# One written schedule for a whole attention and two-expert-layer kernel, counts loaded one expert ahead, and other PSUM banks for the transposes

## Chip, cores and metric

The kernel runs on one core of one Trainium2 chip. The metric is the device time of one execution in microseconds (us), lower is better. The core's engines are named as in the profile: PE (matmuls; PEld is its weight loads), DVE (vector), ACT (scalar), POOL and SP. Each takes its own list of instructions in order, and waits at semaphores that the others raise.

## The reference

```python
# 1. chunked attention (2 batches, 8 heads, 576 rows, head size 64, chunks of 64 rows)
#    softmax(q k^T / 8) v inside each chunk; out as x of 1152 rows of 512
# 2. mixture of 8 experts, one expert for each row
logits = x @ w_gate
expert_idx = np.argmax(logits, axis=1)
...
for i in range(N):
    e = expert_idx[i]
    if counts[e] < capacity:      # capacity = 1152 // 8 * 2 = 288
        disp[e, counts[e]] = x[i]
...
h = np.maximum(np.einsum('ecd,edf->ecf', disp, w1), 0.0)   # 512 -> 1024
y = np.einsum('ecf,efd->ecd', h, w2)                       # 1024 -> 512
out[i] = gate_w[i] * y[expert_idx[i], pos[i]]              # kept rows only, else 0
# 3. four domain experts, every row through each, mixed by domain_probs
for e in range(E):
    h = np.maximum(x @ w1[e], 0.0)
    out += p[:, e:e + 1] * (h @ w2[e])
```

## The kernel before

**Three stages.** The attention stage works through nine tiles of 128 rows and ends with the routing: DVE computes for every expert how many rows it keeps, the lists of row numbers for the gathers (`gidx`), and a row of 17 whole numbers `ovi`: the count of all kept rows, a form for each of eight experts in the order in which they are worked on, and the column at which each expert's rows start. The expert stage (`expert`, `block`) works on one expert after the other. The dense stage (`dense`) sends all rows through the four domain experts.

**Forms and blocks.** How many rows an expert has is known only at run time, so each expert has three blocks of code: block 1 for rows 128 to 255 (form above 2), block 2, called the small block here, for up to 64 rows (form 2 or 3), and block 0 for the first 128 rows, always run. Blocks 1 and 2 stand under `tc.If` (lines 677, 682 and 683), and the next expert under line 728. Every engine takes these branches by itself, from a register loaded from `ovi` by `numbers` (line 549). An engine that skips a block adds to its semaphore what the block would have added, after its own earlier work has ended.

**One block.** All weights and activations are split in a high and a low part (ACT makes the high part, DVE subtracts it from the source to get the low one) and multiplied in three products. On PE a block is: `first(0)`, the 512-wide first layer of one half of the hidden units; half of `first(1)`; `turn(0)`, which transposes the first half by matmuls with the identity; the rest of `first(1)`; `second(0)`, the second layer, which reads `ht`, the turned half after ACT (high, line 596) and DVE (low, line 597); `turn(1)`; the rest of `second`; then the result is turned again (`ty`) and put into `x2`. The turns go through PSUM tiles of the tag `tp`, with two buffers for all blocks; `ys2` are two accumulators, `pg0` one bank for each kind of block, `pg1` one for all: 2 + 2 + 3 + 1 = 8 banks.

**Around the blocks.** `late(k)` ends the splitting of the expert's own second-layer weights: two casts on ACT (line 115) and four subtractions on DVE (`part_lo`, line 119), ahead of the expert's first branch. Between the steps of block 0 the lists in `also` split the next expert's weights, load the one after it, and turn the next expert's gathered rows (`xprep`, lines 538 to 546), through `pg0[1]`, `pg0[2]` and `pg1` (line 701). For the first expert `xprep` runs ahead of its blocks and uses `tp`, `pg0[0]` and `pg1` (line 663).

**What sets the order.** A region under `tc.manual_schedule` is issued as written on the engines it names; outside such a region a scheduler chooses. The attention stage has a region of its own (line 128, all engines), the expert stage one (line 520) and the dense stage one (line 735), the latter two for PE, ACT, DVE and SP.

Of the kernel before, what the change touches and what calls it, by code (L numbers as in the profile page):

```python
# [71 lines left out]
def kernel(ctx: ExitStack, tc: tile.TileContext, kqv_d, wg, w_all, dp, cst, out, cap):  # L72
# [3 lines left out]
    XW = 2 * P + 64  # L76
    assert cap <= XW

    dpool = ctx.enter_context(tc.tile_pool(name="dpool", bufs=1, space=DRAM))
    x_d = dpool.tile([NTOK, DM], F32, name="x_d")  # L80
    meta_d = dpool.tile([NTOK, MC], F32, name="meta_d")
# [43 lines left out]
    with ExitStack() as ast:  # L125
        ap_ = ast.enter_context(tc.tile_pool(name="attn", bufs=2))
        ps = ast.enter_context(tc.tile_pool(name="aps", bufs=1, space=PSUM))
        ast.enter_context(tc.manual_schedule())


        wz = ap_.tile([P, 512], F16, bufs=1, name="wz")
# [385 lines left out]
    def w2(h, part, ff):  # L517
        return hls[2 * h + 1][:, part, ff * DM:(ff + 1) * DM]

    with ExitStack() as est, tc.manual_schedule(engines={ENG.PE, ENG.Activation, ENG.DVE, ENG.SP}):  # L520
        hp_ = est.enter_context(tc.tile_pool(name="mh", bufs=2))
        xtp = est.enter_context(tc.tile_pool(name="mx", bufs=1))
        ps = est.enter_context(tc.tile_pool(name="mps", bufs=1, space=PSUM))

        ys2 = [ps.tile([P, DM], F32, name=f"y{j}") for j in range(2)]


        pg0 = [ps.tile([P, FH], F32, name=f"pg0{j}") for j in range(3)]
        pg1 = ps.tile([P, FH], F32, name="pg1")
        xts = [xt0, xtp.tile([P, 2 * KD * XW], F32R, name="xt1")]  # L530
        xbig = [x[:, 0:4 * KD * P].rearrange("p (a k n) -> p a k n", a=2, k=KD) for x in xts]
        xsmall = [x[:, 4 * KD * P:].rearrange("p (k a n) -> p k a n", a=2, k=KD) for x in xts]
# [5 lines left out]
        def xprep(k, kd, t):  # L538
            for w in range(2):
                nc.tensor.transpose(t[:, w * P:w * P + P], xrs[k % 2][:, w, kd * P:kd * P + P], ident)  # L540
            hi_lo(xbig[k % 2][:, 0, kd], xbig[k % 2][:, 1, kd], t[:, 0:2 * P])
# [6 lines left out]
        def numbers(src, **kw):  # L548
            return nc.values_load_multi_w_load_instructions(src, min_val=0, **kw)[1]

        kept, *form_r = numbers(ovi[0:1, 0:1 + NE], max_val=NTOK)
        o_r = numbers(ovi[0:1, 1 + NE:1 + 2 * NE], engines=(ENG.Activation, ENG.DVE), max_val=NTOK)
        regs = []

        def load(k, j, h):
# [4 lines left out]
        def block(k, w, also=()):  # L560
# [2 lines left out]

            lo, n = wins[w]
            both = n < P
            y = ys2[w % 2]
            hs, ht = {}, {}
            pg = (pg0[w], pg1)

# [19 lines left out]
                nc.scalar.copy(hs[h], pg[h])  # L589

            def turn(h):
                tp = ps.tile([P, NF, n], F32, tag="tp", bufs=2, name="tp")
                for j in range(NF):
                    turned(tp[:, j], hs[h][:, j * P:j * P + P])
                ht[h] = hp_.tile([P, NF, 2, n], F32R, tag="h", name="ht")
                nc.scalar.activation(out=ht[h][:, :, 0], in_=tp, func=ACTF.Relu)  # L596
                nc.vector.scalar_tensor_tensor(out=ht[h][:, :, 1], in0=tp, scalar=0.0, in1=ht[h][:, :, 0].bitcast(F32),  # L597
                                               op0=ALU.max, op1=ALU.subtract)
# [23 lines left out]
            place(4)  # L622
            second(1, range(NF))
            yr = hp_.tile([P, DM], F32, tag="ys", bufs=1, name="yr")
            ty = ps.tile([P, KD, n], F32, tag="tp", bufs=2, name="tp")
            for j in range(2):
                nc.scalar.copy(yr[:, j * 256:j * 256 + 256], y[:, j * 256:j * 256 + 256])
            place(5)
# [22 lines left out]
        def expert(k):  # L651
# [3 lines left out]
            if k == 0:  # L655
                gather(0, (2,))
                gather(1)

                nc.gpsimd.memset(x2[:, :, :, P:NTOK].bitcast(F32), 0.0)
                for h in range(2):  # L660
                    part_lo(0, h)
                for kd in range(KD):
                    xprep(0, kd, ps.tile([P, 512], F32, tag="tp", bufs=2, name="tp") if kd < 2 else (pg0[0], pg1)[kd - 2])
                for h in range(2):
                    part_lo(2, h)
                places()
                regs.extend(numbers(pli[0:1, :], engines=(ENG.SP,), max_val=NE + NDOM - 1))
                chores = list(dense_rows())
                for h in range(2):
                    part_lo(1, h)  # L670
                for j in (0, 2, 1):
                    for h in range(2):
                        load(1, j, h)
            elif k + 2 < NE:
                gather(k + 2)
            late(k)
            with tc.If(form_r[k] > 2):
                block(k, 1)
            if k == 0:
# [18 lines left out]

            def nxt(i, kd):
                if k + 1 < NE:  # L700
                    t = pg1 if len(turns) == KD else pg0[1 + len(turns) % 2]
                    turns.append(t)
                    also[i].append(lambda: xprep(k + 1, kd, t) if kd < KD else xprep_small(k + 1, t))

# [17 lines left out]
            assert len(chores) <= 20  # L722
            block(k, 0, also)
            if k == 0:
                scatter(meta_d, [(posi[:, i:i + 1], meta[:, i]) for i in range(NT)], [])
                nc.gpsimd.dma_start(out=mcol, in_=meta_d.rearrange("(i p) c -> p i c", p=P))
            if k + 1 < NE:
# [4 lines left out]
        late(NE)  # L732


    with ExitStack() as est, tc.manual_schedule(engines={ENG.PE, ENG.Activation, ENG.DVE, ENG.SP}):
        accp = est.enter_context(tc.tile_pool(name="accp", bufs=1))
        hp_ = est.enter_context(tc.tile_pool(name="dh", bufs=2))
        ps = est.enter_context(tc.tile_pool(name="dps", bufs=4, space=PSUM))
# [130 lines left out]
        def pick_last(ws):  # L869
            if len(ws) == 1:  # L870
                return dense(ws[0])
            with tc.If(kept <= LAST + ws[0]) as few:  # L872
                dense(ws[0])
            with few.Else():
                pick_last(ws[1:])
# [46 lines left out]
```

## Time and profile before

| | |
|---|---|
| median of 3 runs | 619.68 us (617.58 to 619.73) |
| the profiled execution | 620.28 us, its span 618.1 us |
| PE busy | 579.5 us, 94% of the span |
| DVE, ACT busy | 296.1 us, 200.9 us |
| mean granted clock of PE | 0.975 of full speed |
| start of the dense stage on PE | 240.21 us |

The profiled execution's time is 2.2 us more than its span, which runs from the first to the last recorded instruction. Routing ends at about 59 us, the expert stage runs to 240 us. With these inputs six experts have rows. In the order worked on their blocks are: 1 and 0; 1, 2 and 0; 0; 2 and 0; 2 and 0; 0. They are called experts 0 to 5 below.

### The profile page before, as it was taken

What the parts mean: (1) busy time and instruction counts of PE and PEld (TensorE: products, weight loads), DVE (VectorE), ACT (ScalarE), POOL (GpSimd) and SP (SyncE); (2) the same over time, 40 slices, a digit from 0 to 9 for tenths busy, and PEclk for the clock granted to TensorE, in tenths of its full rate; (3) what the DMA queues carried; (4) which work ended last, traced back from release to release, by engine and by line L of the source; (5) the groups of instructions that cost most, each with busy time, mean ns of one, the idle gap of its engine ahead of it and who ended that gap; (6) DMA issues with size and microseconds to landing.
All of it is one profiled execution on the core that took longest, in us unless ns stands there. A gap on an engine that the chain in (4) does not pass through costs nothing.

```text
span 618.1 us, 8796 instructions
## 1 busy us (share of the span) xinstructions
PE 579.5 (94%) x3376; PEld 503.6 (81%) x3376; DVE 296.1 (48%) x576; ACT 200.9 (32%) x394; POOL 71.5 (12%) x63
## 2 busy tenths in 40 slices
PE   6998699998797988999999999999999999999995
PEld 3785577776676767989989989989989989989984
DVE  4897828147445376242462452452452452454221
ACT  4785237267454476111211211211211211211110
POOL 3311813202202050000000000000000000000032
PEclk8997799999898999999999999999999999999998
DMA  8782286428727176400120120120220000000022
GB/s 326 258 286 75 60 315 202 114 73 296 262 69 249 46 233 200 186 1 1 68 69 1 68 69 1 69 68 1 69 68 1 2 1 1 1 0 1 1 83 76
DMA packets 17322, 61.36 MB, mean 99 GB/s; under 512 B 2720, under 2 KB 2864, under 8 KB 16624
## 3 DMA queue, kind: packets, MB, share of 16 engines
q1 hardware_dynamic: 14544, 52.95, 25.1%
q0 software_dynamic: 2720, 7.66, 4.1%
q8 instruction: 33, 0.54, 0.4%
q14 instruction: 25, 0.20, 0.1%
HBM read 55.86 MB, written 4.75 MB: 98 GB/s over the span
## 4 chain that ended last, share of the span: by engine, by line
PE 59%; issue 1%; POOL 1%; DVE 0%; POOLq 0%
PE pg L768 30%; PE po L797 20%; PE po L816 8%; POOL out L500 1%; PE po L831 0%; DVE xr L804 0%; POOLq L872 0%; POOLq L500 0%
## 5 line engine op out<-in xcount | busy, mean ns | idle before, releaser
L768 PE MATMUL pg<-x,hl 128*128 128x384 f32 (+1 forms) x1152 | 187.5, 322 | 1.6 <-DVEq L728 1.6
L768 PEld LDWEIGHTS pg<-x,hl 128*128 128x128 f32 x1152 | 184.5, 188 | 3.1 <-issue 1.8
L797 PE MATMUL po<-hl,h 128*128 128x512 f32 (+1 forms) x588 | 137.4, 392 | 0.0
L797 PEld LDWEIGHTS po<-hl,h 128*128 128x128 f32 x588 | 108.6, 188 | 24.6
L119 DVE TENSOR_TENSOR hl<-raw,hl 128x1024 fp32r<-128x1024 f32 x80 | 95.3, 1219 | 24.0 <-ACT hl L115 20.2
L778 ACT ACTIVATE h<-pg 128x384 fp32r<-128x384 f32 x64 | 31.5, 492 | 186.1 <-PE pg L768 185.8
L115 ACT CAST hl<-raw 128x1024 fp32r<-128x1024 f32 x80 | 82.2, 1056 | 0.9 <-DVEq L728 0.9
L779 DVE SCALAR_TENSOR_TENSOR h<-pg,h 128x384 fp32r<-128x384 f32 x64 | 35.6, 557 | 94.2 <-ACT h L778 94.2
L574 PE MATMUL pg<-hl,xt 128*128 128x512 f32 x240 | 65.4, 421 | 3.2 <-PEq L682 1.6
L574 PE MATMUL y<-hl,ht 128*128 128x512 f32 x240 | 65.0, 412 | 1.6 <-DVE ht L597 1.6
L804 DVE SCALAR_TENSOR_TENSOR xr<-po,mcol,xr 128x512 f32<-128x512 f32 (+1 forms) x43 | 31.7, 737 | 59.7 <-PE po L797 59.0
L574 PEld LDWEIGHTS pg<-hl,xt 128*128 128x128 f32 x240 | 45.9, 200 | 14.6 <-issue 5.3
L574 PEld LDWEIGHTS y<-hl,ht 128*128 128x128 f32 x240 | 43.7, 192 | 13.4 <-DVE ht L597 4.4
L816 PE MATMUL po<-h,hl 128*128 128x288 f32 x384 | 51.9, 295 | 0.0
L816 PEld LDWEIGHTS po<-h,hl 128*128 128x128 f32 x384 | 51.3, 189 | 0.0
L775 ACT CAST h<-pg 128x288 fp32r<-128x288 f32 x32 | 12.8, 400 | 97.9 <-DVE pg L773 97.9
L400 POOL DMA_INDIRECT xr<-x_d,gidx x24 | 28.2, 1174 | 127.8 <-PE pg L540 95.4
L825 POOL MEMSET raw<- 128x512 f32 x1 | 0.5, 527 | 268.4 <-DVE hl L119 268.4
L597 DVE SCALAR_TENSOR_TENSOR ht<-tp,ht 128x512 fp32r<-128x512 f32 (+1 forms) x22 | 13.6, 616 | 28.5 <-ACT ht L596 28.4
L822 DVE TENSOR_TENSOR rest<-po,rest 128x288 f32<-128x288 f32 x28 | 12.8, 458 | 26.6 <-PE po L816 26.6
L773 DVE SCALAR_TENSOR_TENSOR pg<-pg,xt 128x288 f32<-128x288 f32 x32 | 22.1, 690 | 1.6 <-PE pg L768 1.6
L776 DVE TENSOR_TENSOR h<-pg,h 128x288 fp32r<-128x288 f32 x32 | 14.7, 459 | 15.4 <-ACT h L775 15.4
(158 smaller groups left out, 393.6 us busy)
## 6 DMA issues: line engine op xcount, KB each, us to landing
raw<-in_w_all SPq DMA_DIRECT2D x72, 512.0 KB, 4.1
kqv<-in_kqv SPq DMA_DIRECT2D x8, 768.0 KB, 8.1
raw<-in_w_all SPq DMA_DIRECT2D x4, 1024.0 KB, 5.7
x_d<-x SPq DMA_DIRECT2D x9, 256.0 KB, 3.1
xt<-meta_d SPq DMA_DIRECT2D x1, 1056.0 KB, 8.5
kqv<-in_kqv SPq DMA_DIRECT2D x3, 256.0 KB
xr<-x_d,gidx POOLq DMA_INDIRECT x24
cc<-in_cst SPq DMA_DIRECT2D x1, 373.5 KB
```

The costliest lines, as they stand in the source:

```text
L115: nc.scalar.copy(hls[j][:, 0, a:b], raws[j][:, a:b])
L119: nc.vector.tensor_tensor(out=hls[j][:, 1, a:b], in0=raws[j][:, a:b], in1=hls[j][:, 0, a:b].bitcast(F32), op=ALU.subtract)
L400: nc.gpsimd.indirect_dma_start(out=xrs[k % 2][0:n, w, :], out_offset=None, in_=x_d[:, :], in_offset=bass.IndirectOffsetOnAxis(ap=ix, axis=0))
L574: nc.tensor.matmul(o, t(a), wt(b), start=start and i == 0, stop=stop and i == len(pairs) - 1)
L768: nc.tensor.matmul(pg[:, 0:n], w1(u % 2, a, kd)[:, ff * P:ff * P + P], x2[:, b, kd, g * GW:g * GW + n], start=c == 0, stop=c == 3 * KD - 1)
L773: nc.vector.scalar_tensor_tensor(out=hs, in0=hs, scalar=0.0, in1=domain(u // NH), op0=ALU.max, op1=ALU.mult)
L776: nc.vector.tensor_tensor(out=h[:, ff, 1, 0:n], in0=hs, in1=h[:, ff, 0, 0:n].bitcast(F32), op=ALU.subtract)
L778: nc.scalar.activation(out=h[:, ff, 0], in_=pg[:, 0:GW], func=ACTF.Relu)
L779: nc.vector.scalar_tensor_tensor(out=h[:, ff, 1], in0=pg[:, 0:GW], scalar=0.0, in1=h[:, ff, 0].bitcast(F32), op0=ALU.max, op1=ALU.subtract)
L797: nc.tensor.matmul(po, h[:, ff, a, tt * P:tt * P + P], w2(u % 2, b, ff)[:, cols], start=c == 0, stop=c == 3 * NF - 1)
L804: nc.vector.scalar_tensor_tensor(out=acc[t][:, cols], in0=po, scalar=pe, in1=acc[t][:, cols], op0=ALU.mult, op1=ALU.add)
L816: nc.tensor.matmul(po[:, 0:W], w2(u % 2, b, ff)[:, d * P:d * P + P], h[:, ff, a, 0:W], start=c == 0, stop=c == 3 * NF - 1)
```

## The change

Four things are changed. One `manual_schedule` for PE, ACT, DVE and SP spans the whole kernel (POOL keeps one in the attention stage). The registers are loaded with the numbers of one expert at a time: the form of expert 0 ahead of the stage, then `count(k + 1)` behind `late(k)` inside expert `k`, one load on every engine and a second one on ACT and DVE; the count of kept rows is loaded behind expert 0's block 0. The PSUM tiles: three `tps`, one for each kind of block, take `turn(0)` and `ty`; `turn(1)` reuses the block's own `pg0`; one accumulator `y` serves all: 3 + 3 + 1 + 1 = 8 banks. `xprep` for the next expert uses `pg0[1]`, `pg0[2]`, `tps[1]`, `tps[2]` and `pg1`, and for expert 0 `tps[0]`, `tps[2]`, `pg0[0]` and `pg1`.

```diff
@@ -76,6 +76,7 @@
     XW = 2 * P + 64
     assert cap <= XW
 
+    ctx.enter_context(tc.manual_schedule(engines={ENG.PE, ENG.Activation, ENG.DVE, ENG.SP}))
     dpool = ctx.enter_context(tc.tile_pool(name="dpool", bufs=1, space=DRAM))
     x_d = dpool.tile([NTOK, DM], F32, name="x_d")
     meta_d = dpool.tile([NTOK, MC], F32, name="meta_d")
@@ -125,7 +126,7 @@
     with ExitStack() as ast:
         ap_ = ast.enter_context(tc.tile_pool(name="attn", bufs=2))
         ps = ast.enter_context(tc.tile_pool(name="aps", bufs=1, space=PSUM))
-        ast.enter_context(tc.manual_schedule())
+        ast.enter_context(tc.manual_schedule(engines={ENG.Pool}))
 
 
         wz = ap_.tile([P, 512], F16, bufs=1, name="wz")
@@ -517,16 +518,17 @@
     def w2(h, part, ff):
         return hls[2 * h + 1][:, part, ff * DM:(ff + 1) * DM]
 
-    with ExitStack() as est, tc.manual_schedule(engines={ENG.PE, ENG.Activation, ENG.DVE, ENG.SP}):
+    with ExitStack() as est:
         hp_ = est.enter_context(tc.tile_pool(name="mh", bufs=2))
         xtp = est.enter_context(tc.tile_pool(name="mx", bufs=1))
         ps = est.enter_context(tc.tile_pool(name="mps", bufs=1, space=PSUM))
 
-        ys2 = [ps.tile([P, DM], F32, name=f"y{j}") for j in range(2)]
 
 
         pg0 = [ps.tile([P, FH], F32, name=f"pg0{j}") for j in range(3)]
+        tps = [ps.tile([P, 512], F32, name=f"tp{j}") for j in range(3)]
         pg1 = ps.tile([P, FH], F32, name="pg1")
+        y = ps.tile([P, DM], F32, name="y")
         xts = [xt0, xtp.tile([P, 2 * KD * XW], F32R, name="xt1")]
         xbig = [x[:, 0:4 * KD * P].rearrange("p (a k n) -> p a k n", a=2, k=KD) for x in xts]
         xsmall = [x[:, 4 * KD * P:].rearrange("p (k a n) -> p k a n", a=2, k=KD) for x in xts]
@@ -548,8 +550,15 @@
         def numbers(src, **kw):
             return nc.values_load_multi_w_load_instructions(src, min_val=0, **kw)[1]
 
-        kept, *form_r = numbers(ovi[0:1, 0:1 + NE], max_val=NTOK)
-        o_r = numbers(ovi[0:1, 1 + NE:1 + 2 * NE], engines=(ENG.Activation, ENG.DVE), max_val=NTOK)
+        kept = []
+        form_r = [*numbers(ovi[0:1, 1:2], max_val=4)]
+        o_r = [0]
+
+        def count(k):
+
+            form_r.extend(numbers(ovi[0:1, 1 + k:2 + k], max_val=4))
+            o_r.extend(numbers(ovi[0:1, 1 + NE + k:2 + NE + k], engines=(ENG.Activation, ENG.DVE), max_val=NTOK))
+
         regs = []
 
         def load(k, j, h):
@@ -563,7 +572,6 @@
 
             lo, n = wins[w]
             both = n < P
-            y = ys2[w % 2]
             hs, ht = {}, {}
             pg = (pg0[w], pg1)
 
@@ -589,7 +597,7 @@
                 nc.scalar.copy(hs[h], pg[h])
 
             def turn(h):
-                tp = ps.tile([P, NF, n], F32, tag="tp", bufs=2, name="tp")
+                tp = (tps, pg0)[h][w][:, 0:NF * n].rearrange("p (f n) -> p f n", f=NF)
                 for j in range(NF):
                     turned(tp[:, j], hs[h][:, j * P:j * P + P])
                 ht[h] = hp_.tile([P, NF, 2, n], F32R, tag="h", name="ht")
@@ -622,7 +630,7 @@
             place(4)
             second(1, range(NF))
             yr = hp_.tile([P, DM], F32, tag="ys", bufs=1, name="yr")
-            ty = ps.tile([P, KD, n], F32, tag="tp", bufs=2, name="tp")
+            ty = tps[w][:, 0:KD * n].rearrange("p (d n) -> p d n", d=KD)
             for j in range(2):
                 nc.scalar.copy(yr[:, j * 256:j * 256 + 256], y[:, j * 256:j * 256 + 256])
             place(5)
@@ -660,7 +668,7 @@
                 for h in range(2):
                     part_lo(0, h)
                 for kd in range(KD):
-                    xprep(0, kd, ps.tile([P, 512], F32, tag="tp", bufs=2, name="tp") if kd < 2 else (pg0[0], pg1)[kd - 2])
+                    xprep(0, kd, (tps[0], tps[2], pg0[0], pg1)[kd])
                 for h in range(2):
                     part_lo(2, h)
                 places()
@@ -674,6 +682,8 @@
             elif k + 2 < NE:
                 gather(k + 2)
             late(k)
+            if k + 1 < NE:
+                count(k + 1)
             with tc.If(form_r[k] > 2):
                 block(k, 1)
             if k == 0:
@@ -698,7 +708,7 @@
 
             def nxt(i, kd):
                 if k + 1 < NE:
-                    t = pg1 if len(turns) == KD else pg0[1 + len(turns) % 2]
+                    t = (pg0[1], pg0[2], tps[1], tps[2], pg1)[len(turns)]
                     turns.append(t)
                     also[i].append(lambda: xprep(k + 1, kd, t) if kd < KD else xprep_small(k + 1, t))
 
@@ -722,6 +732,7 @@
             assert len(chores) <= 20
             block(k, 0, also)
             if k == 0:
+                kept.extend(numbers(ovi[0:1, 0:1], max_val=NTOK))
                 scatter(meta_d, [(posi[:, i:i + 1], meta[:, i]) for i in range(NT)], [])
                 nc.gpsimd.dma_start(out=mcol, in_=meta_d.rearrange("(i p) c -> p i c", p=P))
             if k + 1 < NE:
@@ -732,7 +743,7 @@
         late(NE)
 
 
-    with ExitStack() as est, tc.manual_schedule(engines={ENG.PE, ENG.Activation, ENG.DVE, ENG.SP}):
+    with ExitStack() as est:
         accp = est.enter_context(tc.tile_pool(name="accp", bufs=1))
         hp_ = est.enter_context(tc.tile_pool(name="dh", bufs=2))
         ps = est.enter_context(tc.tile_pool(name="dps", bufs=4, space=PSUM))
@@ -869,7 +880,7 @@
         def pick_last(ws):
             if len(ws) == 1:
                 return dense(ws[0])
-            with tc.If(kept <= LAST + ws[0]) as few:
+            with tc.If(kept[0] <= LAST + ws[0]) as few:
                 dense(ws[0])
             with few.Else():
                 pick_last(ws[1:])
```

DVE, from the end of the routing to expert 0's first rows. `ovi` is the row of 17 numbers, `gp` and `gidx` make the gather lists, `over` is the routing's last PSUM read, `hl` the split weights, `xt` expert 0's turned rows. Before:

```order
L440 TENSOR_TENSOR dt<-tsb 128x8
L549 TENSOR_LOAD ovi
L918 BRANCH_PREFETCH_HINT
L441 TENSOR_TENSOR dt<-dt,thr 128x8
L442 TENSOR_TENSOR tsb<-tsb,dt 128x8
L549 TENSOR_LOAD ovi
L119 TENSOR_TENSOR hl_91<-raw_87,hl_91 128x1024
L443 TENSOR_TENSOR gp<-tsb,sel 128x192
L119 TENSOR_TENSOR hl_91<-raw_87,hl_91 128x1024
L445 TENSOR_REDUCE gidx<-gp 128x24
L447 TENSOR_TENSOR over<-n_ps,st 128x8
L536 TENSOR_TENSOR xt_71<-tp,xt_71 128x256 x2
```

The same place of the change:

```order
L441 TENSOR_TENSOR dt<-tsb 128x8
L442 TENSOR_TENSOR dt<-dt,thr 128x8
L443 TENSOR_TENSOR tsb<-tsb,dt 128x8
L444 TENSOR_TENSOR gp<-tsb,sel 128x192
L446 TENSOR_REDUCE gidx<-gp 128x24
L448 TENSOR_TENSOR over<-n_ps,st 128x8
L551 TENSOR_LOAD ovi
L120 TENSOR_TENSOR hl_93<-raw_89,hl_93 128x1024 x2
L538 TENSOR_TENSOR xt_73<-tp_1010,xt_73 128x256
```

The two loads and the two weight subtractions have moved behind `over`, and of the loads one is left here.

PE, the small block of an expert past the first, with the semaphores waited for; `pg`, `tp` and `y` are the PSUM tiles. Before:

```order
L574 MATMUL pg_1012<-hl_93,xt_71 128x512 x3
L578 MATMUL tp<-cc,hs 128x64 [waits DVE_49,Activation_49]
L578 MATMUL tp<-cc,hs 128x64 x3
L574 MATMUL pg_1012<-hl_93,xt_71 128x512 x4
L574 MATMUL y_1007<-hl_92,ht 128x512 [waits DVE_49]
```

And in the change:

```order
L582 MATMUL pg_1013<-hl_95,xt_73 128x512 x3
L586 MATMUL tp_1012<-cc,hs 128x64 [waits Activation_49]
L586 MATMUL tp_1012<-cc,hs 128x64 x3
L582 MATMUL pg_1013<-hl_95,xt_73 128x512 x4
L582 MATMUL y<-hl_94,ht 128x512 [waits DVE_49]
```

`turn(0)` (lines 578 and 586) no longer waits for DVE; the first product of `second(0)` still does.

DVE in the change, from an expert's `late` to its first branch; line 120 is `part_lo`, line 551 the loads of the next expert's numbers, line 605 the low part of `ht`:

```order
L120 TENSOR_TENSOR hl_94<-raw_90,hl_94 128x1024 x2
L120 TENSOR_TENSOR hl_96<-raw_92,hl_96 128x1024 x2
L551 TENSOR_LOAD ovi
L929 BRANCH_PREFETCH_HINT
L551 TENSOR_LOAD ovi
L687 COMPARE_AND_BRANCH
L605 SCALAR_TENSOR_TENSOR ht<-tp_1011,ht 128x4x128
```

Before, the four subtractions were followed by the branch at once, and the hint stood ahead of them. PE has one such load between line 739 (728 before) and its hint.

## Rows read from the trace of the kernel before

**Rows 1.** The profile's page: engines; the chain that ended last, its first PE step.

```profile
PE 579.5 (94%) x3376; PEld 503.6 (81%) x3376; DVE 296.1 (48%) x576; ACT 200.9 (32%) x394; POOL 71.5 (12%) x63
...
240.21 16.88 PE pg L768 x96
```

**Rows 2.** Waits of PE from 58 to 241 us: us in total, times, longest.

```profile
PE tp L540 <- DVE over L447: 5.0, 1, 5.0
PE tp L578 <- DVEq L677: 4.5, 2, 2.3
...
PE tp L580 <- DVEq L682: 2.7, 2, 1.4
```

**Rows 3.** Stretches with one small block each: experts 1, 3 and 4.

```profile
core 0: us, PE busy (x) PEld busy (x) DVE busy (x) ACT busy (x) POOL busy (x), PEclk, DMA share, GB/s
...
114.70:126.30 11.60, 11.06 (x57) 8.46 (x57) 1.54 (x3) 3.18 (x7) 0.00 (x0) 1.00 0.07 25
...
158.60:174.20 15.60, 12.78 (x57) 9.74 (x57) 6.08 (x7) 4.63 (x9) 2.48 (x2) 0.89 0.59 190
...
189.60:206.70 17.10, 14.31 (x57) 11.14 (x57) 6.08 (x7) 4.57 (x9) 2.41 (x2) 0.80 0.53 176
```

**Rows 4.** Timeline of PE, small blocks: start, us, instruction, idle before and releaser.

```profile
119.66 1.20 PE L574 MATMUL y<-hl,ht 128*128 128x512 f32 x4
...
164.21 1.76 PE L578 MATMUL tp<-cc,hs 128*128 128x64 f32 x8 [2.27 <-DVEq L677]
...
167.58 1.21 PE L574 MATMUL y<-hl,ht 128*128 128x512 f32 x4
...
198.69 1.91 PE L574 MATMUL y<-hl,ht 128*128 128x512 f32 x4
```

**Rows 5.** DVE's branch at line 677 in expert 3 (window 157.5 to 169 us).

```profile
L677 DVEq COMPARE_BRANCH  x1: 56/56/56, 160.7 to 160.7; - x1
L677 DVEq EVENT_SEMAPHORE  x1: 21/21/21, 164.0 to 164.0; - x1
```

**Rows 6.** Expert 2, block 0: DVE's low part and PE's second layer.

```profile
148.89 0.69 DVE L597 SCALAR_TENSOR_TENSOR ht<-tp,ht 128x512 fp32r<-128x512 f32 x1
...
149.74 1.64 PE L574 MATMUL y<-hl,ht 128*128 128x512 f32 x6
```

**Rows 7.** Register loads: ns min/median/max, first and last start in us.

```profile
L549 DVEq TENSOR_LOAD <-ovi x2: 1119/1500/1880, 59.6 to 61.1; - x2
L549 SPq TENSOR_LOAD <-ovi x1: 767/767/767, 59.6 to 59.6; - x1
L549 PEldq TENSOR_LOAD <-ovi x1: 1042/1042/1042, 59.6 to 59.6; - x1
...
L364 SPq TENSOR_LOAD <-e0i x1: 533/533/533, 26.7 to 26.7; - x1
```

**Rows 8.** Timeline of PE, expert 0.

```profile
56.45 4.85 PE L138 MATMUL w_ps<-wz 128*128 128x512 f16 x11
66.31 1.09 PE L540 MATMUL tp<-cc,xr 128*128 128x128 f32 x4 [5.01 <-DVE over L447]
...
77.77 1.43 PE L574 MATMUL y<-hl,ht 128*128 128x512 f32 x5 [1.41 <-DVE ht L597]
```

**Rows 9.** Timeline of DVE, the same stretch.

```profile
63.09 1.22 DVE L119 TENSOR_TENSOR hl<-raw,hl 128x1024 fp32r<-128x1024 f32 x1 [1.82 <-issue]
...
69.03 2.35 DVE L119 TENSOR_TENSOR hl<-raw,hl 128x1024 fp32r<-128x1024 f32 x2
...
77.03 0.68 DVE L597 SCALAR_TENSOR_TENSOR ht<-tp,ht 128x512 fp32r<-128x512 f32 x1
```

**Rows 10.** Busy tenths of the DMA engines, 56 to 76 us in slices of 0.5 us.

```profile
DMA  0000000456872000000000000000230638856052
```

**Rows 11.** Timeline of PE, start of expert 1.

```profile
100.54 4.48 PE L574 MATMUL pg<-hl,xt 128*128 128x512 f32 x18
...
107.26 1.44 PE L574 MATMUL y<-hl,ht 128*128 128x512 f32 x5 [0.17 <-DVE ht L597]
```

## The prediction

> **What bounds the kernel now.** First the page: PE is busy for 94% of the span, and the chain that ended last runs on PE from the first dense matmul at 240.21 us [rows 1]. In the dense stage PE has no gaps that the change could close: its instructions there are the same before and after. So I look only at what lies ahead of 240.21 us, and there at PE's waits, since PE is the engine that the others feed. Three of them count [rows 2]: 5.0 us once, expert 0's first transposes (line 540) waiting for DVE to pass line 447, the routing's last read of PSUM; 4.5 us in two, `turn(0)` of the small blocks (line 578) waiting for DVE's branch at line 677; and 2.7 us in two, `turn(0)` of block 0 in experts 2 and 5 (line 580) waiting for DVE's branch at line 682. The table by stretches shows what the second kind costs in all: the same small block takes 11.60 us in expert 1, where nothing stalls, 15.60 in expert 3 and 17.10 in expert 4 [rows 3]. [...]
>
> **The small blocks, experts 3 and 4.** `tp` was shared with a block that was skipped, so `turn(0)` waited until DVE had skipped it too; with a bank for each kind of block this wait is gone. What is late next is the low part of `ht` on DVE, which `second(0)` needs. DVE's sequencer reaches its branch at 160.7 us, but counts the block as skipped only when the four subtractions of `late` are through, at 164.0 [rows 5]. Then ACT's high part and DVE's low part follow, each on 256 columns and so below the 0.69 us that DVE takes for 512 [rows 6]; with the hand-overs I take 1.1 us for both. So `second(0)` can start at 165.1, 6.5 us after the block's start. PE itself is there earlier: its start, plus one register load, plus the 4.96 us of expert 1 (114.70 to 119.66) [rows 3, 4], makes 164.3. Against 167.58 that is 2.5 us in expert 3, and, with the same 6.5 us from 189.60, 196.1 against 198.69, so 2.6 us in expert 4. The rest of the block takes 6.6 us in experts 1 and 3 and 8.0 in expert 4 (198.69 to 206.70) [rows 3, 4]; with no stall long enough to lower the clock expert 4 gets 1.4 of this back. Sum 6.5 us; bounds 3 (the clock falls all the same) and 7.2 (PE's path alone decides).
>
> **Block 0 of experts 2 and 5.** The same wait goes, 2.7 us in sum, but I cost it at nothing. In expert 2 `second(0)` starts at 149.74, straight behind DVE's low part, 148.89 plus 0.69 [rows 6], and DVE's queue up to it is the same as before: four subtractions, branch, one more subtraction. The stall moves from `turn(0)` to `second(0)`. Bounds: 0 to 2.7 gained.
>
> **Expert 0.** Four things stand ahead of line 447 on DVE and now come behind it: loads of 1.12 and 1.88 us [rows 7] and two subtractions of 1.22 us [rows 9], 5.4 us together. PE's release at 66.31 would move to 60.9. Then the warm-up matmuls decide, which end at 61.3 [rows 8], and after them the gathered rows: the DMA engines are busy until slice 13 of the stretch, 62.5 us [rows 10]. So the transposes start at about 62.6. DVE is the next limit: 60.9, one load (0.75, below), two subtractions, 64.1; four low parts of 256 columns at about 0.4 (an estimate from 0.69 for 512), 65.7. From there its queue to the low part of `ht` is as before, where it began at 69.03 [rows 9]. So `second(0)` comes 3.3 us earlier, at 74.5 instead of 77.77 [rows 8]. PE gets there some 6.7 us after its own start at about 64.5, as in expert 1 [rows 11], and now idles over 3 us. After 2.27 us of that kind experts 3 and 4 lost a further 1.7 to 3.2 us to the lower clock (the whole loss, 4.0 and 5.5 us, less the stall) [rows 3, 4]. I take 2.0, and a gain of 1.3; bounds 0 and 3.3.
>
> **The loads.** Before, DVE and ACT made two and the others one, ahead of expert 0; now PE makes 8 and DVE 14 in this execution. The trace has no load of one number from `ovi`. Nearest rows: nine numbers take 0.77 us on SP and 1.04 on PE, and one number took 0.53 on SP [rows 7]; I take 0.75 for PE and DVE, with 0.53 and 1.04 (on DVE 1.88) as bounds. On DVE and ACT the two loads of an expert stand behind the work of `late` and ahead of the branch. DVE's sequencer had 3.3 us to spare there [rows 5], and even the two dearest loads of DVE make 3.0, so they are covered, if a load starts while the engine still works. It does on PE: its load began at 59.6 us, within the warm-up matmuls (56.45 to 61.3) [rows 7, 8]. Without that cover each pair would delay `second(0)` of every expert. On PE the load stands right at the expert's start, where the sequencer is not ahead. In experts 2 to 5 the wait for DVE's low part covers 0.75 us. In expert 1 two loads meet (`kept` and the next form): 1.5 us, of which only the 0.17 us that `second(0)` waited [rows 11] are free: minus 1.3, bounds 0.9 and 1.9. On SP and POOL a load of this kind stands among transfers that are issued an expert ahead; nothing of it reaches PE.
>
> [...]
>
> **The other edits.** The single region leaves every list ahead of line 440 and in the dense stage as it was, so it costs nothing beyond the moves counted. One accumulator `y` for all blocks is rewritten only after a whole first layer (4.48 us [rows 11]), long after ACT has copied it out. The `xprep` that now waits for DVE to skip block 1 comes behind `turn(0)`, when DVE has just done so; bounds 0 to 0.5 us in experts 2 and 5, inside the stall that stays.
>
> **Sum.** 1.3 (expert 0) minus 1.3 (expert 1) plus 2.5 and 4.0 (experts 3 and 4) is 6.5 us. From the profiled 620.28 us that leaves 613.8; the profiled execution was 0.6 above the median, so I expect a median of 613.2 us.
>
> **Rivals.** *The clock stays low.* PE still idles before `second(0)` in five experts. If the lower level comes back in expert 4 (1.4) and in expert 3 (1.7), and expert 0 pays 3.2 instead of 2.0, the gain is 2.2 us: 617.5. For it: idle of this kind was followed by the lower clock in experts 3 and 4; against it: in experts 2 and 5 it was shorter and nothing followed.
> *The loads are not covered (slower).* If a load on DVE starts only when the engine's queue has run empty, the branch comes later by a pair of loads in each of six experts, and every `second(0)` waits for it. With 1.1 us for each load 2.2 a pair, 13 in all, of which expert 1's 1.3 is already counted: 12 more than the sum, 625. It turns the sign when a pair puts more than about 1.3 us on the path. Against it: PE's load among running matmuls, and the 3.3 us. For it: DVE's two loads before were followed by 1.82 us of idle [rows 9], and nothing shows one under long DVE work. [...]
> *More than forecast.* No lower clock in expert 0 and the cheapest loads: 9 us, 610.6.
> *It doesn't do what it says.* Some other shared buffer keeps `turn(0)` or the high part of `ht` behind DVE, so that the small blocks stall as before: only the two first experts change and cancel out, 619.5.
>
> **How the numbers follow.** Forecast 0.57 (gain 4.5 to 8), clock stays low 0.18, more 0.09, loads not covered 0.09, not as it says 0.07. The range of 608.8 to 618.8 leaves out the uncovered loads and most of the last case. A difference below 0.5% (3.1 us) can't be told from none here. Faster by more: the forecast, more than forecast, and half of the low clock, 0.76. Within: the other half, most of the last case, a little of the loads, 0.16. Slower: 0.08.
>
> **What would show it.** Right: no wait of PE on DVE's branch at `turn(0)`; small blocks of experts 3 and 4 at about 13 us each and granted clock near 1.00; expert 0's transposes at about 62.6 us and its `second(0)` at 74.5 behind a longer wait for `ht`; one PE gap of about 2 us at expert 1; experts 2 and 5 as long as before; the dense stage starting at about 233.7 us and lasting as long. Wrong: DVE idle between `late` and its branch (the loads), a low clock in experts 3 and 4, or a load on PE far beyond 1 us.

## The result, and the profile after

The changed kernel takes 610.37 us (median of 4 runs, 608.91 to 611.91), the kernel before 619.09 beside it (4 runs, 617.58 to 619.73): a ratio of 0.9863, with a 95% interval of 0.9831 to 0.9895. The forecast was 613.2 us and a range of 608.8 to 618.8. The profiled execution took 610.78 us. What stands below compares its trace with that of before.

The page of the changed kernel, and from its chain the first matmul of the dense stage:

```profile
span 609.0 us, 8833 instructions
PE 575.9 (95%) x3376; PEld 500.9 (82%) x3376; DVE 296.4 (49%) x576; ACT 200.6 (33%) x394; POOL 70.2 (12%) x63
...
231.30 16.88 PE pg L779 x96
```

The dense stage starts at 231.30 us instead of 240.21 [rows 1] and lasts 377.7 us instead of 377.9 (span less start). So 8.9 of the 9.1 us of difference between the spans lie ahead of it, where PE now waits as follows (58 to 241 us; us in total, times, longest):

```profile
PE y L582 <- DVE ht L605: 4.6, 3, 2.5
PE pg L582 <- PEq L687: 3.1, 3, 1.1
PE tp L588 <- ACT yr L635: 2.8, 8, 0.5
PE tp L542 <- DMA xr<-x_d,gidx: 2.2, 2, 1.2
...
PE pg L582 <- PEq L692: 1.3, 1, 1.3
```

The three waits of [rows 2] are gone. What is late next is the low part of `ht` on DVE (line 605), the gather of expert 0's rows, and PE's own branches at the start of an expert (`PEq`). The small blocks of experts 1, 3 and 4, and the start of expert 5, in the table by stretches (the number behind the busy times of the five engines is the granted clock):

```profile
112.60:124.20 11.60, 11.04 (x57) 8.46 (x57) 1.54 (x3) 3.18 (x7) 0.00 (x0) 1.00 0.01 3
156.50:169.10 12.60, 11.02 (x57) 8.42 (x57) 5.76 (x7) 4.03 (x8) 1.98 (x2) 1.00 0.68 227
184.90:197.40 12.50, 10.97 (x56) 8.39 (x57) 5.72 (x7) 3.98 (x8) 1.94 (x2) 1.00 0.78 226
213.40:216.80 3.40, 3.39 (x9) 2.70 (x10) 3.40 (x5) 1.24 (x2) 2.79 (x3) 0.59 0.71 195
```

Against [rows 3] the small blocks of experts 3 and 4 are 3.0 and 4.6 us shorter and run at the full clock (1.00, where it read 0.89 and 0.80). Expert 5 now begins partly at the lower one (0.59 in this stretch; the start of expert 5, 222.2 to 225.6 us, read 1.00 before).

PE in the small block of expert 3, and DVE there (start, us, instruction, idle before it and its releaser):

```profile
159.38 1.05 PE L586 MATMUL tp<-cc,hs 128*128 128x64 f32 x8
160.24 1.18 PE L582 MATMUL pg<-hl,xt 128*128 128x512 f32 x4
162.48 1.20 PE L582 MATMUL y<-hl,ht 128*128 128x512 f32 x4 [1.07 <-DVE ht L605]
...
156.79 4.62 DVE L120 TENSOR_TENSOR hl<-raw,hl 128x1024 fp32r<-128x1024 f32 x4
162.00 0.42 DVE L605 SCALAR_TENSOR_TENSOR ht<-tp,ht 128x256 fp32r<-128x256 f32 x1 [0.59 <-ACT ht L604]
```

`turn(0)` (line 586) has no idle time ahead of it, where [rows 4] had 2.27 us; what is left of the wait, 1.07 us, stands ahead of `second(0)`, behind DVE's four subtractions and the two parts of `ht`. DVE's branch and the register loads:

```profile
L687 DVEq COMPARE_BRANCH  x1: 63/63/63, 159.0 to 159.0; - x1
L687 DVEq EVENT_SEMAPHORE  x1: 21/21/21, 161.5 to 161.5; - x1
...
L551 DVEq TENSOR_LOAD <-ovi x2: 307/308/309, 158.1 to 158.6; - x2
...
L551 DVEq TENSOR_LOAD <-ovi x14: 298/306/555, 61.6 to 215.2; - x14
L551 PEldq TENSOR_LOAD <-ovi x8: 297/308/483, 60.7 to 211.8; - x8
```

A load of one number takes 0.31 us in the median (the first one on DVE 0.56). DVE's two loads in expert 3 start at 158.1 and 158.6, while its subtractions run (156.79 to 161.41), and its branch is read 2.5 us before the block counts as skipped (161.5): in [rows 5] these were 3.3 us, so the loads used up cover, not time.

Expert 0 on PE:

```profile
62.47 0.30 PE L542 MATMUL tp<-cc,xr 128*128 128x128 f32 x1 [1.03 <-DMA xr<-x_d,gidx]
63.93 0.90 PE L542 MATMUL tp<-cc,xr 128*128 128x128 f32 x3 [1.16 <-DMA xr<-x_d,gidx]
...
75.23 1.44 PE L582 MATMUL y<-hl,ht 128*128 128x512 f32 x5 [2.55 <-DVE ht L605]
```

The transposes wait for the gather, and `second(0)` waits 2.55 us for DVE, where [rows 8] had 5.01 and 1.41.

The stretches between fixed points of PE's timeline, in us, for all the traces of this study (worked out from their starts; routing's end is the start of DVE's `dt` from `tsb`, line 440 or 441):

```
                                before  changed   e1     e2     e3     e4     e5     e6     e7     e8
routing ends at                  59.48   60.54   59.07  58.44  61.92  62.30  60.86  59.51  59.89  59.09
to expert 0, block 0             26.43   22.83   26.41  24.76  23.98  24.73  23.93  22.98  22.42  22.67
expert 0, block 0                14.63   15.45   14.64  14.64  15.48  14.63  15.47  14.65  14.63  15.46
expert 1, three blocks           41.25   41.27   41.17  41.25  41.28  41.16  41.30  41.15  41.36  41.35
expert 2                         16.84   16.39   16.46  16.87  16.74  16.42  15.62  16.31  15.13  16.37
expert 3, small block            15.54   12.58   12.90  14.22  16.79  12.91  11.53  13.08  11.76  12.59
expert 3, block 0                15.42   15.88   15.45  15.44  15.80  15.47  15.80  15.39  15.40  15.86
expert 4, small block            17.11   12.47   12.89  16.99  15.25  12.89  11.48  12.97  11.68  12.49
expert 4, block 0                15.57   16.00   15.58  15.58  16.01  15.57  15.99  15.57  15.57  15.98
expert 5                         17.94   17.89   17.38  17.93  17.49  17.39  16.37  17.40  16.33  17.89
routing's end to dense stage    180.73  170.76  172.88 177.68 178.82 171.17 167.49 169.50 164.28 170.66
dense stage to end of span      377.89  377.70  379.85 377.68 377.86 377.83 380.25 377.99 379.93 379.35
```

From the routing's end the change saves 9.97 us: 3.60 up to expert 0's block 0, 2.50 in expert 3, 4.21 in expert 4, 0.45 in expert 2 and 0.05 in expert 5, less 0.82 in expert 0's block 0 and 0.02 in expert 1. About one of them is given back because the routing ended 1.06 us later; e8 shows below that this is not the change's. By the medians the change is worth 8.7 us.

### The profile page after: what moved, and what is told of

It is laid out like the page before. It is cut to its first block, busy times and chain, and to the rows that moved or that the text cites. A ratio compares the mean times of both kernels' runs of the same rounds, so it can differ in the third digit from the quotient of the medians.

```text
span 609.0 us, 8833 instructions
## 1 busy us (share of the span) xinstructions
PE 575.9 (95%) x3376; PEld 500.9 (82%) x3376; DVE 296.4 (49%) x576; ACT 200.6 (33%) x394; POOL 70.2 (12%) x63
## 4 chain that ended last, share of the span: by engine, by line
PE 59%; issue 1%; POOL 0%; POOLq 0%; DVE 0%
PE pg L779 30%; PE po L808 21%; PE po L827 8%; POOL out L501 0%; PE po L842 0%; POOLq L929 0%; DVE xr L815 0%; POOLq L883 0%; POOLq L501 0%
## 5 line engine op out<-in xcount | busy, mean ns | idle before, releaser
L582 PE MATMUL pg<-hl,xt 128*128 128x512 f32 x240 | 63.5, 414 | 5.6 <-PEq L687 3.1
L597 ACT COPY hs<-pg 128x512 f32<-128x512 f32 x22 | 13.0, 590 | 25.3 <-PE pg L582 16.6
```

The costliest lines, as they stand in the source:

```text
L582: nc.tensor.matmul(o, t(a), wt(b), start=start and i == 0, stop=stop and i == len(pairs) - 1)
```

## The experiments

Each time is a median; ratios are to the kernel before, measured beside it, with the 95% interval. Single executions lie up to 4.5 us from their median, so the rows of the table decide on single steps. Four kernels took the change apart, then three tried what follows from it, and one repeats it.

**e1: the banks alone** (kernel before with this):

```diff
-        ys2 = [ps.tile([P, DM], F32, name=f"y{j}") for j in range(2)]
+        tps = [ps.tile([P, 512], F32, name=f"tp{j}") for j in range(3)]
+        y = ps.tile([P, DM], F32, name="y")
-                tp = ps.tile([P, NF, n], F32, tag="tp", bufs=2, name="tp")
+                tp = (tps, pg0)[h][w][:, 0:NF * n].rearrange("p (f n) -> p f n", f=NF)
...
```

> The kernel before with the new PSUM banks alone (three tp banks, one y bank, second turn into pg0), loads and schedule spans as before. Theory A, that the banks alone make the gain in the small blocks: small block of expert 3 about 12.6 us long (15.5 before), of expert 4 about 12.5 (17.1 before), expert 0 as before (its transposes still wait about 5 us for DVE), whole kernel 8 us faster than before, 611 us (by the forecast's own terms, 2.5 + 4.0, 612.6). Rival: the wait for the skipped block's branch on DVE is only carried by another tile of the same turn (hs or ht), and the small blocks get shorter only where DVE's queue got shorter too, which needs the spans and the loads: then the small blocks stay within 1 us of 15.5 and 17.1 and the time is 617 to 620.

Measured: 613.09 us, ratio 0.9918 (0.9887 to 0.9948). The small blocks:

```profile
157.70:170.60 12.90, 11.02 (x56) 8.35 (x56) 6.08 (x7) 4.41 (x9) 2.36 (x2) 1.00 0.71 228
186.10:199.00 12.90, 11.07 (x57) 8.40 (x57) 6.08 (x7) 4.36 (x8) 2.31 (x2) 1.00 0.79 239
...
231.90:235.30 3.40, 3.35 (x11) 3.38 (x12) 3.01 (x3) 1.99 (x2) 1.06 (x1) 0.55 0.51 162
```

Both are 12.90 us long, with nothing else changed: the banks make the gain there, 2.64 and 4.22 us, and 7.85 in all up to the dense stage. The rival falls. The time is 2 us above the expected 611. In the profiled execution (613.71 us) the dense stage was 2.0 us longer than before and began at the lower clock (0.55, last row), which it did not do in the trace of the kernel before (1.00 from 240.2 to 243.6 us); whether the other executions did it too is not shown.

**e2: the single span alone** (kernel before with this, and without the two later spans):

```diff
+    ctx.enter_context(tc.manual_schedule(engines={ENG.PE, ENG.Activation, ENG.DVE, ENG.SP}))
...
-        ast.enter_context(tc.manual_schedule())
+        ast.enter_context(tc.manual_schedule(engines={ENG.Pool}))
```

> The kernel before with one schedule span for PE, ScalarE, VectorE and SyncE alone. Only VectorE's order changes: the end of the routing (to the tile over) comes ahead of the number loads and of two part_lo. Theory A: expert 0's first transposes wait for the gather instead of VectorE and start about 4 us earlier, but VectorE has all its work still ahead of the second halves of block 1, less the 1.4 us that it idled for the transposes, so second(0) moves by 1.4 us and the kernel is 1.4 us faster (617.7), up to 3.4 if the low clock after the 5 us wait goes too (615.7); experts 2 to 5 as before. Rival: the whole shift of expert 0 in the changed kernel (3.6 us) is the span's: 615.5.

Measured: 617.66 us, ratio 0.9976 (0.9951 to 1.0002). Expert 0's block 0 came 1.67 us earlier, near theory A's 1.4 and far from 3.6. The rest of its 3.05 us lies in expert 3's small block:

```profile
155.90:170.20 14.30, 11.46 (x57) 8.36 (x57) 6.08 (x7) 4.66 (x9) 2.49 (x2) 1.00 0.66 207
185.60:202.60 17.00, 14.19 (x56) 11.07 (x57) 6.08 (x7) 4.56 (x9) 2.41 (x2) 0.80 0.60 173
```

PE stood still for up to 2.3 us in both blocks, as before; but only the second one fell to the lower clock (0.80). The edit did nothing there: these 1.3 us are clock (1.00 in the first block, 0.89 before). At the full clock the block takes 14.22 us with the old banks (here) and 12.90 with the new ones (e1). So the shorter wait itself is worth 1.3 us, and what the banks save beyond that depends on whether the clock falls behind the wait, as in the second block here (17.00 us at 0.80). By the medians the span alone can't be told from no change.

**e3: the loads alone** (kernel before with this):

```diff
-        kept, *form_r = numbers(ovi[0:1, 0:1 + NE], max_val=NTOK)
+        form_r = [*numbers(ovi[0:1, 1:2], max_val=4)]
...
             late(k)
+            if k + 1 < NE:
+                count(k + 1)
```

> The kernel before with the numbers loaded one expert ahead alone. Theory A: in expert 0 VectorE's loads of 9 and 8 numbers (3.1 us with what surrounds them) become one of about 0.3 us, and two of 0.3 us come behind the first part_lo of late: second(0) about 2.2 us earlier. In experts 1 to 5 the two loads lengthen late on VectorE by 0.6 us, and in the old banks the wait of the turned array grows by that: +0.6 us each in experts 3 and 4, +0.5 at a boundary elsewhere: together the kernel is within 1.5 us of before (618 to 620). Theory of the forecast (loads of 0.75 us, all covered but two on TensorE, lower clock unchanged): 2.4 - 1.3 = 1.1 us faster, 618. Rival: the loads are free past expert 0: 616.9.

Measured: 616.63 us, ratio 0.9968 (0.9939 to 0.9997). Expert 0 gains 2.45 us (2.2 expected), its block 0 loses 0.85, and the blocks 0 of experts 3 and 4 lose 0.4 each. The added 0.6 us of stall that theory A expected on DVE in experts 3 and 4 is not there: PE's waits for the skipped block there were 4.4 us in sum (4.5 before [rows 2]). In that point theory A was wrong, and the forecast right: the loads are covered on DVE. What they cost stands on PE. The median lies at the rival's 616.9, but the loads are not free past expert 0, as the three longer blocks show. The small blocks of experts 3 and 4 changed by +1.25 and -1.86 us, with granted clocks of 0.80 and 0.89 instead of 0.89 and 0.80: these 0.6 us are no gain of the loads.

**e4: banks and span, all 17 numbers loaded ahead of expert 0** (the changed kernel with e3's edit undone).

> The changed kernel with the 17 numbers loaded at once ahead of expert 0, as before. Theory A: expert 0 gives back 2.2 us of its 3.6; the 0.8 us between second(0) of expert 0 and expert 1, and about 0.45 us at the boundaries of experts 2 to 4, are not paid any more, and the stalls of 1.0 us that VectorE's late leaves in the small blocks get 0.6 us shorter: 2.2 - 0.8 - 1.3 - 1.2, about 1 us faster than the changed kernel to no change (609 to 610.5). Theory of the forecast: loading ahead is worth 2.2 to 2.4 us in expert 0 and costs 1.3: 611.5. Rival: without the split, VectorE is late for the whole of expert 0 and the low clock comes with it: 613 or more.

Measured: 611.98 us, ratio 0.9894 (0.9843 to 0.9945). DVE's loads and what came behind them:

```profile
L551 DVEq TENSOR_LOAD <-ovi x2: 1105/1489/1873, 63.3 to 64.6; - x2
...
66.54 2.36 DVE L120 TENSOR_TENSOR hl<-raw,hl 128x1024 fp32r<-128x1024 f32 x2 [2.83 <-issue]
```

DVE had nothing queued ahead of these loads, so it stood for 2.83 us, and expert 0 gives back 1.90 of its 3.60. In return expert 0's block 0 is 0.82 shorter, and expert 5 0.50. Up to the dense stage splitting the loads is worth only 0.4 us (171.17 against 170.76). The two kernels were not measured side by side, and their times overlap (609.6 to 616.0 here), so the medians don't tell whether it is worth 0.4 or 1.6. The rival's lower clock did not come: from `second(0)` of expert 0 to block 0 PE takes 8.14 us, as in the changed kernel.

**e5: two of `late`'s subtractions one block earlier, each with the weight transfer behind it** (the changed kernel with this):

```diff
-            if k:
-                for h in range(2):
-                    part_lo(1, h)
-                    load(k + 1, 1, h)
...
             hi(4, 1, 0)
             hi(4, 1, 1)
+            lo(4, 1, 0)
+            lo(4, 1, 1)
```

> The changed kernel with two of the four subtractions of late (part_lo(1, h), with the load of the next weights behind each) moved into block 0 of the expert before, behind its last part_hi, where VectorE stands idle. Theory A: what is left of the small blocks' stall is VectorE's late (4.6 us ahead of the low part of ht); with 2.3 us of it gone second(0) waits for nothing in experts 2 to 5: block 0 of expert 2 15.9 us long instead of 16.4, the small blocks 11.6 instead of 12.5, expert 5 about 16.5 instead of 17.4 to 17.9: together about 3.5 us faster than the changed kernel, 607. Rival: the two transfers that now start earlier, or the longer VectorE queue behind second(0), delay something in block 0 (its transposes through tps[1], tps[2]) and eat the gain: block 0 becomes 0.5 us longer or more and the kernel is within 1 us of the changed one.

Measured: 608.98 us, ratio 0.9825 (0.9780 to 0.9870). No wait for `ht` is left in experts 2 to 5, and the blocks have the expected lengths: 15.62, 11.53, 11.48 and 16.37 us. These four are 4.33 us shorter than in the changed kernel. Of that 1.1 us went in expert 0, at the lower clock, and 2.6 in the dense stage, where about 1.6 are the lower clock (its first 48 matmuls take 10.13 us, 8.56 in e7):

```profile
75.12 2.50 PE L582 MATMUL y<-hl,ht 128*128 128x512 f32 x5 [2.13 <-DVE ht L605]
...
75.10:78.50 3.40, 3.38 (x10) 2.79 (x11) 0.00 (x0) 0.00 (x0) 2.16 (x3) 0.50 0.92 289
78.50:81.90 3.40, 3.40 (x15) 2.69 (x15) 0.69 (x1) 0.60 (x1) 0.00 (x0) 1.00 1.04 335
228.30:231.70 3.40, 3.35 (x11) 3.38 (x12) 0.00 (x0) 0.00 (x0) 0.00 (x0) 0.56 1.03 312
```

The five matmuls behind expert 0's wait take 2.50 us here and 1.44 in the changed kernel, whose wait was longer (2.55). In the dense stage's first 3.4 us ACT and DVE stood still (0.00 busy, last row), as they do from 226 to 228 us in e7 below, and PE then waited 0.33 us for DVE's `h`.

**e6: expert 0's form alone, all the other numbers at once behind its `late`** (the changed kernel with this):

```diff
-            form_r.extend(numbers(ovi[0:1, 1 + k:2 + k], max_val=4))
-            o_r.extend(numbers(ovi[0:1, 1 + NE + k:2 + NE + k], engines=(ENG.Activation, ENG.DVE), max_val=NTOK))
+            if k == 1:
+                nums = numbers(ovi[0:1, 0:1 + NE], max_val=NTOK)
+                kept.append(nums[0])
+                form_r.extend(nums[2:])
+                o_r.extend(numbers(ovi[0:1, 2 + NE:1 + 2 * NE], engines=(ENG.Activation, ENG.DVE), max_val=NTOK))
...
-                kept.extend(numbers(ovi[0:1, 0:1], max_val=NTOK))
```

> The changed kernel, but the numbers of experts 1 to 7 and the kept count are loaded at once, at the place where expert 1's were loaded (behind expert 0's late); expert 0's form still comes alone. Theory A: a register load is free where the engine's queue holds work beyond it (VectorE: 2.9 us of loads under 4.6 us of subtractions; TensorE waits for VectorE at this place anyhow), and costs its time where the engine's queue is empty (2.8 us of idle in the kernel that loads all ahead of expert 0; about 0.4 us on TensorE at every expert's start in the changed kernel). So expert 0 stays at 22.8 us from the routing's end to its block 0, its block 0 gets 0.8 us shorter, the later boundaries 0.3 to 0.4 each, of which the stalls in experts 3 to 5 take back most: 1 to 1.5 us faster than the changed kernel, 609. Rival, the forecast's 'not covered': a load on VectorE starts only when the queue has run empty: expert 0's second(0) about 3 us later and the kernel 612 to 613.

Measured: 609.83 us, ratio 0.9852 (0.9818 to 0.9886). DVE's loads of one, nine and seven numbers and its work around the last:

```profile
L551 DVEq TENSOR_LOAD <-ovi x3: 564/872/1639, 60.5 to 70.0; - x3
...
69.08 4.64 DVE L120 TENSOR_TENSOR hl<-raw,hl 128x1024 fp32r<-128x1024 f32 x4
73.64 0.68 DVE L608 SCALAR_TENSOR_TENSOR ht<-tp,ht 128x512 fp32r<-128x512 f32 x1
```

The last load starts at 70.0 us, under four subtractions that run from 69.08, and the low part of `ht` follows these at once, at 73.64. So 2.5 us of loads cost DVE nothing here, where 3.0 us of them cost 2.83 in e4: the rival is refuted. By its trace e6 is 1.26 us shorter than the changed kernel up to the dense stage, as expected (the times of the two overlap): 0.80 in expert 0's block 0 and 0.49 in expert 5, which starts at the full clock here (1.00 from 211.6 to 215.0 us).

**e7: e5 and e6 together.**

> Both at once: part_lo(1, h) moved into the block before, and the numbers of experts 1 to 7 loaded at once under expert 0's late. Theory A: with VectorE's stall gone nothing takes back what TensorE saves at the boundaries, so it is 3.5 + 0.8 + 5 x 0.35, about 6 us faster than the changed kernel: 604.5. Rival: the boundary's 0.4 us is the branch and not the load, and the sum is that of the two runs alone, 4.5 us at most: 606 or more.

Measured: 605.54 us, ratio 0.9761 (0.9728 to 0.9795): faster than both kernels (the changed one, again beside it in e8, 611.84). Up to the dense stage it is 6.48 us shorter than the changed kernel, a little over theory A's 6. The rival falls: without a load on PE there, block 0 of experts 3 and 4 takes 15.40 and 15.57 us again, as before the change, so the 0.4 us were the load's. The dense stage is 2.2 us longer, at the full clock (1.00 from 224.2 to 262.0 us), and this is a wait that the changed kernel does not have:

```profile
224.17 8.56 PE L779 MATMUL pg<-x,hl 128*128 128x384 f32 x48 [1.55 <-DVEq L739]
234.85 8.59 PE L779 MATMUL pg<-x,hl 128*128 128x384 f32 x48 [2.12 <-DVE h L790]
...
230.88 2.00 ACT L116 CAST hl<-raw 128x1024 fp32r<-128x1024 f32 x2 [7.64 <-SPq L739]
...
L739 SPq EVENT_SEMAPHORE  x8: 17/17/17, 229.4 to 231.1; - x8
...
L739 SPq COMPARE_BRANCH  x2: 49/60/70, 223.4 to 231.2; - x2
...
226.00:228.00 2.00, 2.00 (x13) 2.00 (x12) 0.00 (x0) 0.00 (x0) 0.00 (x0) 1.00 0.95 322
```

ACT waits 7.64 us for SP, which reads the branch of the experts that have no rows at 223.4 us and counts them as skipped only from 229.4 to 231.1; the DMA engines are 95% busy up to 228 us (the last but one number of the last row). So the weight transfers look like the next bound at this place; no run tested it.

**e8: the changed kernel again.**

> The changed kernel once more, as it is, beside the others on their chip. Theory A: the routing's end (60.5 us in the changed kernel's first trace, 59.5 before) moves by some us from execution to execution of the same instructions, and the stretch of lower clock in expert 5 (213.4 to 216.8) comes at another place or not at all: then the time from the routing's end to the dense stage, without such a stretch, is about 170.2 us, and the median again about 610. Rival: the lower clock in expert 5 belongs to the change and is there again, at the same matmuls.

Measured: 611.84 us (607.35 to 614.61), ratio 0.9874 (0.9830 to 0.9918). The routing ended at 59.09 us instead of 60.54, with the same instructions; over the ten traces it lies between 58.44 and 62.30. This end goes with the granted clock from 10 to 30 us, in the attention stage (changed, e4, e8):

```profile
10.00:30.00 20.00, 18.45 (x182) 14.29 (x184) 14.10 (x51) 11.88 (x37) 7.93 (x8) 0.85 0.76 279
...
10.00:30.00 20.00, 18.52 (x160) 13.98 (x162) 12.86 (x46) 10.64 (x34) 6.74 (x7) 0.76 0.73 275
...
10.00:30.00 20.00, 18.68 (x196) 14.67 (x191) 15.83 (x56) 13.43 (x44) 8.23 (x8) 0.91 0.85 326
```

That clock orders the six traces in which it was read: where it is 0.91 (before, e2, e8) the routing ends at 58.44 to 59.48 us, at 0.85 (changed) at 60.54, at 0.79 (e3) at 61.92, at 0.76 (e4) at 62.30. From the routing's end to the dense stage the two traces of the changed kernel differ by 0.10 us. On the low clock in expert 5 the rival was right:

```profile
211.90:215.30 3.40, 3.40 (x10) 2.73 (x11) 3.40 (x5) 1.20 (x2) 2.79 (x3) 0.65 0.69 194
...
229.80:233.20 3.40, 3.40 (x11) 3.40 (x12) 3.00 (x3) 1.98 (x2) 0.00 (x0) 0.53 0.30 108
```

It is there again, at the same matmuls, and costs 0.5 us (17.89 against 17.39 in e4). The second row, at the start of the dense stage, has no counterpart in the changed kernel's first trace: that one changes from execution to execution, and the dense stage is 1.7 us longer with it (379.35 against 377.70).

## Why the prediction was right, and where its terms were off

The sign, the place and the mechanism held; the predicted 6.5 us were 9.97 in the trace, counted from the routing's end, and 8.7 by the medians. The time lies in the range, but the gain lies above the 4.5 to 8 us that the forecast's own case allowed. By the steps of the prediction:

- **Small blocks, 2.5 and 4.0 us.** Measured 2.50 and 4.21 over each expert, and by the banks alone (e1) 2.64 and 4.22 in the block itself. In the changed kernel the blocks themselves gained 2.96 and 4.64, of which the longer blocks 0 gave back 0.46 and 0.43; that the sums over the experts came out this close is in part luck. `second(0)` started 6.00 and 5.90 us after the block, against 6.5: in expert 3 DVE counted the skipped block 5.0 us after the start instead of 5.4, and what stands behind that took 1.0 instead of 1.1. The 1.4 us of lower clock in expert 4 came back too. But not each such stall brings them: e2 has the same two stalls (2.3 us) and one lower stretch (1.00 and 0.80), in e3 expert 3 has the lower clock of the two (0.80 and 0.89).
- **Experts 2 and 5, nothing.** The wait left `turn(0)` as said, but only a part of it went to `second(0)` (0.32 us in expert 5 of e1); another stands ahead of the next expert's first transposes, for DVE's branch (0.49 and 0.25 us in e1), and the two experts got 0.38 and 0.56 us shorter (e1). In expert 5 the change's low clock took its share back.
- **Expert 0, 1.3 us = 3.3 earlier, less 2.0 for the lower clock.** This is the term that was mis-sized. The shift was 3.6 us, and the lower clock cost nothing: from `second(0)` to block 0 there are 8.14 us both before and after (77.77 to 85.91, 75.23 to 83.37), though PE stood for 2.55 us. The single parts explain the shift: 1.67 by the span (e2) and 2.45 by the loads (e3) when each stands alone, 1.70 by banks and span and 1.90 by the loads on top of them (e4). The charge was not invented, it is just not sure to fall: behind 2.13 us of the same wait in e5 the stretch took 9.67 us (75.12 to 84.79), 1.5 more. I had taken one outcome of a thing that varies as a fixed price; of the six traces with a wait of 2 us or more at this place (changed, e3 and e5 to e8) only e5 shows the charge.
- **The loads: covered on DVE, 1.3 us on PE.** The cover is shown by e6 against e4 (2.5 us of loads under 4.64 us of subtractions and no wait; 3.0 us of them and 2.83 us of idle). The price of a load was taken as 0.75 us, from rows of nine numbers and of one on SP; a load of one number takes 0.31 us in the median on PE and DVE. But there are more of them on PE's path than I counted: not only the two ahead of expert 1 (0.82 us in expert 0's block 0, of which 0.36 come back in the next block, 13.82 us instead of 14.18) but one at every later boundary (about 0.4 us each, experts 1, 3 and 4), of which a following stall took back 0.3 to 0.4. With banks and span in place, the loads cost 1.49 us from expert 0's block 0 to the dense stage (147.93 us in the changed kernel, 146.44 in e4), 0.5 of it with the low clock in expert 5. So 1.3, which the forecast charged to expert 1 alone, was near the truth by luck: the one gap of about 2 us that was to show it there is 0.71 us long.
- **The other edits, nothing.** Nothing in the traces speaks against it: with the new banks, `y` among them, expert 1 takes 41.17 us (e1) and 41.25 before, and from the routing's end to expert 0's block 0 e1 is as long as before.

The sum of the terms' errors is 2.3 us in expert 0, 0.4 in expert 2, 0.2 in expert 4 and 0.5 around expert 1, which makes the missing 3.5. Of the rivals "more than forecast" came nearest, by its own condition: no lower clock in expert 0, and cheap loads (610.6 us).

Open: what decides whether PE runs at the lower clock behind a wait. The length of the wait does not (2.13 us with it in e5, 2.55 and 2.8 without in the changed kernel and e3). Expert 5's stretch came in both traces of the changed kernel and in none of the others; e4 and e6, which have no load on PE at that place, are free of it (the 18 matmuls there take 4.44 and 4.45 us, 5.98 and 5.97 in the changed kernel), but so are e3 and e5 (4.44 and 4.45), which have one and the same gap ahead of the block (1.30 and 1.28 us, 1.28 in both traces of the changed kernel).

## What to carry to other kernels

Here a PSUM buffer shared with a block that was skipped made `turn(0)` wait up to 2.27 us until DVE had skipped that block, and the new banks alone, one for each kind of block, took 7.85 us off the time up to the dense stage (e1): try that before anything finer. In these runs 2.5 us of register loads cost DVE nothing under 4.64 us of queued subtractions (e6), and 3.0 us of them cost 2.83 where its queue was empty (e4); so put them behind long instructions and not ahead of a stage. Nine and seven numbers at once did no harm there (e6). When such a wait goes, look for the queue that is late next: here moving two subtractions of that queue into an idle stretch gave, together with the loads in one place, another 6.5 us up to the dense stage (e7).

## What the runs showed of the hardware

- One number costs 0.28 to 0.31 us to load, in the median of each engine of the changed kernel (0.27 to 0.56 in all); nine cost 0.76 (SP, e6) to 1.12 (DVE, before); the second of two loads in a row on DVE, of eight numbers, takes 1.87 to 1.88 (e4, before).
- Instructions that are the same in all ten traces end the routing anywhere from 58.44 to 62.30 us; in the six in which the granted clock from 10 to 30 us was read, the later the lower it was (0.91 down to 0.76).
- The granted clock fell behind a 2.13 us wait (0.50 in e5) and not behind one of 2.55 us at the same instructions (changed); it read 0.59 behind a gap of 1.28 us at the start of expert 5 (changed), where the 18 matmuls behind it took 5.98 us, and behind the same gap in e5 the same 18 took 4.45.
